# Attention and a rational MoE layer on one core: one store per bank at the end, low weight parts made in place, another order of banks at the start

## The chip, the cores and the metric

The kernel runs on one core of a Trainium2 chip. The metric is the device time of one execution in microseconds. PE is the matrix engine (TensorE), DVE the vector engine (VectorE), ACT the scalar engine (ScalarE), POOL is GpSimd and SP the sync engine, which only issues transfers. PSUM, where matmuls write, has eight banks of 512 fp32 columns by 128 partitions.

## What is computed

Attention over 8 batches, 8 heads, 576 tokens and a head size of 64, in two forms that are added, and then a layer with a rational activation over the 4608 tokens:

```python
def _attn_ref(q, k, v):              # (8, 8, 576, 64)
    q_d, k_d, v_d = (mean over groups of 4 tokens)
    out_up = np.repeat(softmax(q_d @ k_d.T / 8) @ v_d, 4, axis=2)
    mask = np.abs(pos[:, None] - pos[None, :]) < 4
    out_local = softmax(where(mask, q @ k.T / 8, -1e9)) @ v
    return out_up + out_local

def _moe_ref(x, w_in, w_out, a, b):  # (4608, 512), (512, 2048), (2048, 512)
    h = x @ w_in
    P = a[0] + a[1] * h + a[2] * h**2 + a[3] * h**3
    Q = 1.0 + abs(b[0]) * abs(h) + abs(b[1]) * h**2
    return (P / (Q + 1e-06)) @ w_out
```

## The kernel before

The tokens form nine blocks of 512: the first 512 tokens of each batch, and one block of the 64 remaining tokens of all eight batches. A block is worked off in 16 steps, one per 128 columns of `w_in` (an "fc"). Step n has three parts: `h_part` writes h(n) into one PSUM bank (PE), `middle` makes the activation from it (four ACT operations that read the bank, two more, and seven DVE operations), which leaves a high part `gh` and a low part `gl` (tiles g0 to g3), and `o_part`, called o(n), multiplies them by the matching 128 rows of `w_out` and adds into four banks, `ob` (banks 4 to 7), over the 16 steps. o(n) stands two steps behind h(n). At the end of a block `store` copies the four banks to SBUF and issues their stores.

Products run as three passes of a rounded format (fp32r): high times high, low times high, high times low. So every weight pair of two fc (128 x 1024 elements) exists as a high part `wh` and a low part `wl`; `weights` makes them from 64-bit words that SP loads (tiles sx, sl): ACT scales a word (line 367), DVE puts the two halves together (370, 373), ACT casts the high part (403) and DVE subtracts to get the low part (406). `w_out` takes this way. `w_in` does not at once: in block 0 (`NAT` = 16 steps) h is one pass of plain fp32 from the exact weights `wb`, with x in fp32 (line 911), four matmuls of 512 columns. After every second step `parts` turns the exact pair that block 0 no longer needs into `wh` and `wl` for the later blocks: before, `wb` lies in the place of `wh`, ACT writes the negated rounded value to `wl` (428), a transfer issued by POOL adds `wb` to it (415), and ACT rounds `wb` in place (430).

The attention of a batch goes by pairs of heads: local scores, a maximum, exponentials (tile el), the same for the pooled form (tiles pq, epc), a division, transposes on PE and copies by ACT back to SBUF (et, eptc), products with v and, by `put_x`, the sum of both forms into x (tile xf). Two pairs make a `Half`; `turn` is the transposes, `weight` the products with v (part_b, part_a). Batch 0 has nothing to overlap with and runs first, its halves over four pairs of banks `bp[0]` to `bp[3]`; batch 1 runs beside block 0, batch 2 beside block 1, and so on.

The order of instructions on every engine is fixed beforehand: each piece of work is handed to a planner (`Plan`) with an assumed duration, its readers and writers, and a due time, and the planner lists the pieces engine by engine. Due times come from constants at the end of the file (`H0`, `H_FIRST`, `H_STEP`, `QUAD_GAP`). While PE would wait in batch 0 the planner's caller adds `warm` matmuls (line 1128) that write an idle bank and are not used.

Of the kernel before, what the change touches and what calls it, by code (L numbers as in the profile page):

```python
# [9 lines left out]
F32 = mybir.dt.float32  # L10
# [9 lines left out]
DM, DF = 512, 2048  # L20
# [167 lines left out]
def attention_moe(  # L188
# [49 lines left out]
    for name, parts in (("wl", low2), ("wh", high2)):  # L238
        for w in range(2):
            for f in range(0, NFC, 2):  # L240
                t = put(f"{name}{w}_{f}", [P, 2, NCC, P], F32R)
                parts[w].append(t)
                if (parts is high2) == (f < (0 if w else NAT)):
                    bits2[w][f // 2] = put(f"wb{w}_{f}", [P, 2, NCC, P], I32, t.at)
    high, low = (
        [[part(x[w][f // 2], x[w][f // 2].ap[:, f % 2], f % 2 * 4 * DM, 4 * DM) for f in range(NFC)] for w in range(2)]
# [104 lines left out]
    def weights(w, f, spot, due=None):  # L351
        st = spot.ap.rearrange("p n (c f two) -> p n c f two", two=2, c=NCC)
        whole = f < (0 if w else NAT)
        added = not whole and ADDED[w] <= f < NFC - 2
        room = low2[w][f // 2 + 1] if added else (high2 if whole else low2)[w][f // 2]
        word = aside[w][f // 2 + 1] if added else bits2[w][f // 2]

        def load():
            src = w_in[f : f + 2] if w == 0 else w_out[f * P : (f + 2) * P, :].rearrange("(n p) x -> n p x", p=P)
            nc.sync.dma_start(out=spot.ap, in_=src.rearrange("n p x -> p n x"))  # L360

        word1, word0 = st[:, :, :, :, 1], st[:, :, :, :, 0]
# [14 lines left out]

        add("SP", 3.3, load, (), (spot,), due=due)
        add("ACT", 0.94, scaled, (spot,), (spot,))
        add("DVE", 0.6, upper, (spot,), (room,))  # L380
        add("DVE", 1.13, lower, (spot, room), (room,))
        if added:
            hi, lo = high2[w][f // 2], low2[w][f // 2]
            if f >= CAST:
                add(
                    "POOL", 1.0, lambda: nc.gpsimd.dma_start(out=flat2(hi), in_=flat2(word).bitcast(F32)),
                    (room,), (hi,), lag=CLAG, load=3.0,
                )
            else:
                add("ACT", 0.88, lambda: nc.scalar.copy(out=hi.ap, in_=word.ap.bitcast(F32)), (room,), (hi,))  # L390
            if NEG:
                add(
                    "DVE", 0.6,
                    lambda: nc.vector.tensor_single_scalar(
                        out=lo.ap, in_=hi.ap.bitcast(F32), scalar=-1.0, op=ALU.mult
                    ), (hi,), (lo,),
                )
            else:
                add("ACT", 0.88, lambda: nc.scalar.mul(out=lo.ap, in_=hi.ap.bitcast(F32), mul=-1.0), (hi,), (lo,))
            accumulate(lo, word, room)  # L400
        elif not whole:
            hi, lo = high2[w][f // 2], low2[w][f // 2]
            add("ACT", 0.88, lambda: nc.scalar.copy(out=hi.ap, in_=word.ap.bitcast(F32)), (lo,), (hi,))
            add(
                "DVE", 1.13,
                lambda: nc.vector.tensor_tensor(
                    out=lo.ap, in0=word.ap.bitcast(F32), in1=hi.ap.bitcast(F32), op=ALU.subtract
                ),
                (lo, hi), (lo,),
            )  # L410
# [8 lines left out]
    def parts(w, f, due=None):  # L419

        hi, lo, word = high2[w][f // 2], low2[w][f // 2], bits2[w][f // 2]
        exact = word.ap.bitcast(F32)
        if DEFER == 2:
            add("ACT", 0.88, lambda: nc.scalar.mul(out=lo.ap, in_=exact, mul=-1.0), (hi,), (lo,), due=due)
            accumulate(lo, word, hi, due)
            add("DVE", 0.6, lambda: nc.vector.tensor_copy(out=hi.ap, in_=exact), (hi,), (hi,), due=due)
        elif DEFER == 1:
            add("ACT", 0.88, lambda: nc.scalar.mul(out=lo.ap, in_=exact, mul=-1.0), (hi,), (lo,), due=due)
            accumulate(lo, word, hi, due)
            add("ACT", 0.88, lambda: nc.scalar.copy(out=hi.ap, in_=exact), (hi,), (hi,), due=due)  # L430
        else:
            add("ACT", 0.88, lambda: nc.scalar.mul(out=lo.ap, in_=exact, mul=-1.0), (hi,), (lo,), due=due)
            add(
                "DVE", 1.13, lambda: nc.vector.tensor_tensor(
                    out=lo.ap, in0=exact, in1=lo.ap.bitcast(F32), op=ALU.add
                ), (hi, lo), (lo,), due=due,
            )
            add("DVE", 0.6, lambda: nc.vector.tensor_copy(out=hi.ap, in_=exact), (hi,), (hi,), due=due)
# [172 lines left out]
    def normalize(c):  # L611
# [10 lines left out]
                    scale=sm[:, NW + i : NW + i + 1],  # L622
                )

        if c.b in EP_DVE:
            add(
                "DVE", 0.6,
                lambda: nc.vector.tensor_tensor(
                    out=c.pool.e.ap[:, :, :, c.odd, :QC], in0=c.pool.e.ap[:, :, :, c.odd, :QC],
                    in1=sm[:, NW:].unsqueeze(2).unsqueeze(3).broadcast_to([P, NQ, NK, QC]), op=ALU.mult,  # L630
                ),
                (*c.eproom, s.sm), c.eproom,
            )
        else:
            add("ACT", 0.92, pooled, (*c.eproom, s.sm), c.eproom, lag=LATE)
# [263 lines left out]
    def h_part(n, f):  # L899
# [5 lines left out]
        if n < NAT:  # L905

            x = xsf[blk.slot][1]
            for c in range(NCC):

                def issue(c=c):  # L910
                    nc.tensor.matmul(  # L911
                        ph.ap, lhsT=bits2[0][fc // 2].ap[:, fc % 2, c, :].bitcast(F32), rhs=x.ap[:, c, :],
                        start=(c == 0), stop=(c == NCC - 1),
                    )

                add("PE", 0.858, issue, (high[0][fc], part(x, None, 4 * c * t, 4 * t)), (ph,), due=due_h(n) + 0.05 * c)
            return
        for part_ in range(3):
            i, j = PROD[part_]
# [81 lines left out]
    def store(k):  # L1001
        blk = blocks[k]
        due = due_h(blk.first + blk.nstep + 2)
        for sub in range(blk.nsub):
            po = ob[sub]
            hi, osb = blk.x[0], xsf[blk.slot][0]
            room = part(hi, None, 4 * sub * DM, 4 * DM)
            osb = flat(osb.ap)[:, sub * DM : (sub + 1) * DM]
            if k == len(blocks) - 1 and sub % 2:
                add("DVE", 0.6, lambda osb=osb, po=po: nc.vector.tensor_copy(out=osb, in_=po.ap), (po,), (room,), due=due)  # L1010
            else:
                add("ACT", 0.49, lambda osb=osb, po=po: nc.scalar.copy(out=osb, in_=po.ap), (po,), (room,), due=due)
            if blk.b is not None:
                rows = [(blk.b, sub * P, P)]
            else:
                rows = blk.rows[2 * sub : 2 * sub + 2]
            for i, (b, t, n) in enumerate(rows):
                add(
                    "SP", 0.7,
                    lambda osb=osb, b=b, t=t, n=n, i=i: nc.sync.dma_start(  # L1020
                        out=out[b * S + t : b * S + t + n, :], in_=osb[i * n : (i + 1) * n, :]
                    ),
                    (room,), (), due=due + 2,
                )
# [9 lines left out]


    due0 = due_h(0) - 4.0
    firsts = [Half(0, q, due0 - 10.0 * (1 - q)) for q in range(2)]
    c0 = [c for x in firsts for c in x.cs]
    for c, due in zip(c0, LOADS[0]):
        load_qk(c, due)  # L1040
# [20 lines left out]
        half_.turn(bp[a], bp[b], bp[a])  # L1061
        half_.weight(bp[b], bp[a])

    begin(c0[0], 0)
    begin(c0[1], 1)
    begin(c0[2], 3)
    for c in c0[:2]:
        pool_qk(c)
    firsts[0].pooled(bp[2])
    begin(c0[3], 0)  # L1070
    for c in c0[2:]:
        pool_qk(c)
    firsts[1].pooled(bp[1])
    finish(firsts[0], 2, 3)
    finish(firsts[1], 0, 1)
    for w, f, spot in chunks[len(early) :]:
        weights(w, f, spot)

# [105 lines left out]
ADDED = (99, 99)
# [67 lines left out]
```

## Time and profile before

| | |
|---|---|
| time, three runs | 961.51, 961.99, 962.8 us; median 961.99 |
| the profiled execution | 961.83 us, span 960.0 us |
| granted clock of PE | 0.996 in the mean |
| busy | PE 939.1, weight load 738.1, DVE 843.4, ACT 812.4, POOL 121.1 us |
| instructions | 19318 |
| moved | read 74.37 MB, written 9.44 MB |

The span goes from the first to the last instruction; the execution's own time is 1.8 us longer. In a row of the profile stand the line, the engine, the operation, what it writes and reads (tile names, without numbers), the shape, the count, and behind the bar busy time, mean of one, and the idle time before it with what ended it. PEld is the loading of weights into PE, which runs beside the matmuls. A busy PE includes pipelining, so its busy time is not its work. An fp32 matmul (line 911) shows as two records.

### The profile page before, as it was taken

To read this page: it belongs to the slowest core of one execution; us is meant where nothing else is said; L and a number is where in the kernel's file an instruction comes from. 1 tells how busy PE (TensorE), PEld (TensorE's weight loads), DVE (VectorE), ACT (ScalarE), POOL (GpSimd) and SP (SyncE) were. 2 spreads that over 40 slices of the span, in tenths; PEclk is the share of its full clock that TensorE was granted. 3 is DMA by queue.
4 is the path that set the end of the run, shared out by engine and by line. 5 is a ranking of instruction groups with operands and counts; after the bars stand their busy time and mean duration, and the time that the engine had idled before them with its cause. 6 is when DMAs were issued, how large, how long until landed. Compare 5 with 4: busy or idle time off the path is not lost.

```text
span 960.0 us, 19318 instructions
## 1 busy us (share of the span) xinstructions
PE 939.1 (98%) x7184; PEld 738.1 (77%) x7184; DVE 843.4 (88%) x1430; ACT 812.4 (85%) x1992; POOL 121.1 (13%) x144
## 2 busy tenths in 40 slices
PE   7899999999999999999999999999999999999996
PEld 5565667878878788888878887878878888888885
DVE  7799999898889889798988898898979899988885
ACT  4799999999798888979797979888897977778674
POOL 1212022121102020212121210212021000000000
PEclk9999999999999999999999999999999999999999
DMA  9997477363333444343343423434332010001001
GB/s 298 279 326 194 105 191 175 84 123 84 72 99 62 108 69 110 63 107 58 94 93 76 89 58 110 74 93 77 102 57 51 1 45 1 1 1 45 1 0 45
DMA packets 44318, 89.26 MB, mean 93 GB/s; under 512 B 4992, under 2 KB 25856, under 8 KB 44224
## 3 DMA queue, kind: packets, MB, share of 16 engines
q1 hardware_dynamic: 25344, 63.52, 20.1%
q0 software_dynamic: 18880, 24.50, 17.7%
q8 instruction: 57, 0.93, 0.4%
q14 instruction: 37, 0.30, 0.1%
HBM read 74.37 MB, written 9.44 MB: 87 GB/s over the span
## 4 chain that ended last, share of the span: by engine, by line
PE 58%; ACT 20%; DVE 17%; issue 4%; DVEq 0%; POOL 0%; ACTq 0%; POOLq 0%
PE psum L989 26%; PE psum L923 25%; ACT m L936 6%; ACT el L739 4%; ACT epc L603 2%; DVE g L963 2%; DVE m L966 2%; DVE m L971 2%; ACT gb L936 2%; DVE g L972 2%; PE psum L911 2%; DVE m L951 1%; ACT epc L620 1%; DVE m L956 1%; DVE m L960 1%
## 5 line engine op out<-in xcount | busy, mean ns | idle before, releaser
L989 PE MATMUL psum<-wh,g 128*128 128x512 f32 x1152 | 392.2, 402 | 3.2 <-DVE g L972 1.4
L936 ACT ACTIVATE m<-psum,cf 128x512 f32<-128x512 f32 x288 | 216.0, 754 | 62.6 <-PE psum L923 54.8
L923 PE MATMUL psum<-xs,wh 128*128 128x512 f32 x1024 | 260.6, 394 | 0.0
L989 PEld LDWEIGHTS psum<-wh,g 128*128 128x128 f32 x1152 | 213.6, 188 | 55.7 <-DVE g L972 5.0
L989 PE MATMUL psum<-wl,g 128*128 128x512 f32 x576 | 224.3, 390 | 0.0
L923 PEld LDWEIGHTS psum<-xs,wh 128*128 128x128 f32 x1024 | 189.5, 188 | 42.2 <-issue 1.8
L963 DVE TENSOR_TENSOR g<-m,m 128x512 fp32r<-128x512 f32 x144 | 99.3, 690 | 65.7 <-ACT m L936 60.3
L923 PE MATMUL psum<-xs,wl 128*128 128x512 f32 x512 | 138.3, 392 | 0.0
L989 PEld LDWEIGHTS psum<-wl,g 128*128 128x128 f32 x576 | 108.2, 188 | 24.7 <-issue 2.2
L936 ACT ACTIVATE gb<-psum,cf 128x512 f32<-128x512 f32 x144 | 116.8, 811 | 10.4 <-PE psum L989 10.3
L936 ACT ACTIVATE gb<-m,cf 128x512 f32<-128x512 f32 x144 | 108.5, 754 | 19.6 <-DVE m L951 12.8
L474 POOL DMA_DIRECT2D pq<-in_qkp_dram x84 | 74.4, 929 | 383.5 <-DMA pq<-in_qkp_dram 305.0
L951 DVE SCALAR_TENSOR_TENSOR m<-m,cf,m 128x512 f32<-128x512 f32 x144 | 107.3, 745 | 6.9 <-ACT m L936 6.9
L923 PEld LDWEIGHTS psum<-xs,wl 128*128 128x128 f32 x512 | 95.4, 188 | 20.4 <-issue 0.6
L936 ACT ACTIVATE m<-gb 128x512 f32<-128x512 f32 x144 | 93.8, 651 | 19.4 <-DVE m L956 17.7
L960 DVE TENSOR_TENSOR m<-m,gb 128x512 f32<-128x512 f32 x144 | 99.0, 688 | 7.4
L966 DVE SCALAR_TENSOR_TENSOR m<-m,g 128x512 f32<-128x512 f32 x144 | 99.3, 690 | 3.4
L972 DVE TENSOR_TENSOR g<-m,m 128x512 fp32r<-128x512 f32 x144 | 98.7, 685 | 4.0
L971 DVE TENSOR_TENSOR m<-m,m 128x512 f32<-128x512 f32 x144 | 99.1, 688 | 2.6
L956 DVE TENSOR_TENSOR m<-m,m 128x512 f32<-128x512 f32 x144 | 98.5, 684 | 2.8 <-ACT m L936 2.8
L936 ACT ACTIVATE m<-psum 128x512 f32<-128x512 f32 x144 | 88.8, 617 | 0.0
L474 POOL DMA_DIRECT2D vpc<-in_vp_dram x42 | 34.9, 830 | 216.3 <-DMA vpc<-in_vp_dram 201.8
(78 smaller groups left out, 950.2 us busy)
## 6 DMA issues: line engine op xcount, KB each, us to landing
qk<-in_qk_dram SPq DMA_DIRECT2D x32, 590.0 KB, 3.9
pq<-in_qkp_dram POOLq DMA_DIRECT2D x84, 144.0 KB, 3.4
vw<-in_vw_dram SPq DMA_DIRECT2D x32, 320.0 KB, 4.0
out_dram<-xf SPq DMA_DIRECT2D x32, 256.0 KB, 2.4
vpc<-in_vp_dram POOLq DMA_DIRECT2D x42, 168.0 KB, 3.7
sx<-in_w_in_dram SPq DMA_DIRECT2D x5, 1024.0 KB, 12.2
sl<-in_w_out_dram SPq DMA_DIRECT2D x4, 1024.0 KB, 12.5
sx<-in_w_out_dram SPq DMA_DIRECT2D x4, 1024.0 KB, 6.5
```

Of the source, the lines that this page charges most:

```text
L474: lambda d=dst, x=x: nc.gpsimd.dma_start(out=d.ap, in_=x, accum_op=ALU.add),
L739: nc.scalar.activation(out=e[:, n], in_=e[:, n], func=AF.Exp, bias=nm[:, n : n + 1], scale=scale, accum_out=sm[:, n : n + 1],)
L923: nc.tensor.matmul(ph.ap[:, f * t : (f + 1) * t], lhsT=(high, low)[j][0][fc].ap[:, c, :], rhs=blk.x[i].ap[:, c, :] if blk.b is not None el ...
L936: add("ACT", cost, lambda: nc.scalar.activation(out=out_.ap, in_=in_, func=func, **kw), (room_in, cf, *more), (out_,))
L951: lambda: v.scalar_tensor_tensor(out=tb.ap, in0=tq.ap, scalar=b1, in1=tb.ap, op0=ALU.mult, op1=ALU.add),
L956: add("DVE", 0.61, lambda: v.tensor_tensor(out=ta.ap, in0=ta.ap, in1=tq.ap, op=ALU.mult), (ta, tq), (ta,))
L960: add("DVE", 0.61, lambda: v.tensor_tensor(out=ta.ap, in0=ta.ap, in1=u.ap, op=ALU.add), (ta, u), (ta,))
L963: add("DVE", 0.61, lambda: v.tensor_tensor(out=gh.ap, in0=ta.ap, in1=tq.ap, op=ALU.mult), (ta, tq), (gh,))
L966: lambda: v.scalar_tensor_tensor(out=tb.ap, in0=tb.ap, scalar=CONE, in1=gh.ap.bitcast(F32), op0=ALU.add, op1=ALU.mult),
L971: add("DVE", 0.61, lambda: v.tensor_tensor(out=tb.ap, in0=ta.ap, in1=tb.ap, op=ALU.subtract), (ta, tb), (tb,))
L972: add("DVE", 0.61, lambda: v.tensor_tensor(out=gl.ap, in0=tb.ap, in1=tq.ap, op=ALU.mult), (tb, tq), (gl,))
L989: nc.tensor.matmul(ob[sub].ap, lhsT=g[i].ap[:, f0 : f0 + P], rhs=flat((high, low)[j][1][fc].ap), start=(fc == 0 and m == 0), stop=(fc == N ...
```

## The change

Four things change.

1. `store` for the last block: ACT copies the left half of each output bank and DVE the right half, and each bank's 128 rows, which belong to two batches, go out in one transfer instead of two, on the queues of SP and ACT in turn (sub 0 and 2, sub 1 and 3).
2. `DEFER` goes from 1 to 4: the exact pair lies in the place of `wl`, ACT casts it to `wh` (now line 424), and DVE subtracts in place (line 426). There is no transfer.
3. Batch 0's pairs use other banks (`BANKS`), h(0) and h(1) stand in banks 2 and 3 instead of 7 and 5 (`HFIRST`), where h(2) and h(3) follow, and due times differ.
4. `EP_DVE` is asked by pair instead of by batch, with the four pairs of batch 0 in it.

```diff
@@ parts
+        if DEFER == 4:
+            add("ACT", 0.88, lambda: nc.scalar.copy(out=hi.ap, in_=exact), (lo,), (hi,), due=due)
+            add(
+                "DVE", 1.13, lambda: nc.vector.tensor_tensor(
+                    out=lo.ap, in0=exact, in1=hi.ap.bitcast(F32), op=ALU.subtract
+                ), (lo, hi), (lo,), due=due,
+            )
@@ store
-            if k == len(blocks) - 1 and sub % 2:
-                add("DVE", 0.6, lambda osb=osb, po=po: nc.vector.tensor_copy(out=osb, in_=po.ap), (po,), (room,), due=due)
...
+            if blk.b is None:
+                lo, hi = (osb[:, i * DM // 2 : (i + 1) * DM // 2] for i in range(2))
+                plo, phi = (po.ap[:, i * DM // 2 : (i + 1) * DM // 2] for i in range(2))
+                rooms = [part(room, None, i * 2 * DM, 2 * DM) for i in range(2)]
+                add("ACT", 0.3, lambda o=lo, p=plo: nc.scalar.copy(out=o, in_=p), (po,), (rooms[0],), due=due)
+                add("DVE", 0.34, lambda o=hi, p=phi: nc.vector.tensor_copy(out=o, in_=p), (po,), (rooms[1],), due=due)
+                dst = out.rearrange("(b s) d -> b s d", s=S)[2 * sub : 2 * sub + 2, FULL:, :]
+                queue, engine = ("SP", nc.sync) if sub % 2 == 0 else ("ACT", nc.scalar)
                 add(
-                    "SP", 0.7,
...
+                    queue, 0.7, lambda e=engine, d=dst, o=osb: e.dma_start(out=d, in_=o), (room,), (),
+                    due=due + 2 + sub,
                 )
@@ batch 0
-    begin(c0[0], 0)
-    begin(c0[1], 1)
-    begin(c0[2], 3)
...
-    firsts[0].pooled(bp[2])
-    begin(c0[3], 0)
...
-    firsts[1].pooled(bp[1])
-    finish(firsts[0], 2, 3)
-    finish(firsts[1], 0, 1)
+    begin(c0[0], turns[0])
+    begin(c0[1], turns[1])
...
+    firsts[0].pooled(bp[pooled[0]])
...
+    begin(c0[3], turns[3])
...
+    firsts[1].pooled(bp[pooled[1]])
+    finish(firsts[0], *ends[0])
+    finish(firsts[1], *ends[1])
@@ constants
-HFIRST = (7, 5)
+HFIRST = (2, 3)
-H0 = 14.21
+H0 = 20.18
...
+BANKS = ((0, 1, 3, 2), (2, 3), ((0, 1), (2, 3)))
...
-DEFER = 1
+DEFER = 4
```

What the constants do to the order shows in the lists of the engines. ACT in batch 0, before, from the pooled exponentials of half 0 (epc0) on; el2 and el3 are the local exponentials of pairs 2 and 3, epc1 the pooled ones of half 1, et and eptc the copies of transposes of half 0:

```order
L603 ACTIVATE epc0_162,sm1_157<-psum,nm1_153 128x3x48 x3
L553 ACTIVATE el2_178<-psum 128x5x64
L553 ACTIVATE el3_183<-psum 128x5x64
L553 ACTIVATE el2_178<-psum 128x5x64
L553 ACTIVATE el3_183<-psum 128x5x64
L367 ACTIVATE sx0_189<-sx0_189 128x1024
L796 COPY eptc0_163<-psum 112x384
L796 COPY et0_168<-psum 128x512
L796 COPY et1_173<-psum 128x512
L796 COPY eptc0_163<-psum 112x384
L603 ACTIVATE epc1_185,sm2_158<-psum,nm2_154 128x3x48 x3
L603 ACTIVATE epc1_185,sm3_159<-psum,nm3_155 128x3x48 x3
```

ACT at the same place now, from the first copy on:

```order
L803 COPY eptc0_163<-psum 112x384
L803 COPY et0_168<-psum 128x512
L803 COPY et1_173<-psum 128x512
L803 COPY eptc0_163<-psum 112x384
L560 ACTIVATE el3_183<-psum 128x5x64
L610 ACTIVATE epc1_185,sm2_158<-psum,nm2_154 128x3x48 x3
L803 COPY et0_168<-psum 128x128
L803 COPY et1_173<-psum 128x128
L803 COPY eptc0_163<-psum 112x96
L560 ACTIVATE el3_183<-psum 128x5x64
L367 ACTIVATE sx1_190<-sx1_190 128x1024
L610 ACTIVATE epc1_185,sm3_159<-psum,nm3_155 128x3x48 x3
```

Pair 3 (el3, sm3) has moved behind the copies of half 0, and the pooled exponentials of half 1 are no longer made in one piece ahead of the last three copies.

DVE at the start of block 1, before; m, g and gb are tiles of the activation:

```order
L963 TENSOR_TENSOR g0_138<-m0_132,m4_136 128x512
L406 TENSOR_TENSOR wl1_14_78<-wb1_14_79,wh1_14_103 128x1024
L966 SCALAR_TENSOR_TENSOR m2_134<-m2_134,g0_138 128x512
L956 TENSOR_TENSOR m1_133<-m1_133,m5_137 128x512
L971 TENSOR_TENSOR m2_134<-m0_132,m2_134 128x512
L960 TENSOR_TENSOR m1_133<-m1_133,gb1_143 128x512
L972 TENSOR_TENSOR g2_140<-m2_134,m4_136 128x512
L963 TENSOR_TENSOR g1_139<-m1_133,m5_137 128x512
```

DVE at the same place now:

```order
L978 TENSOR_TENSOR m2_134<-m0_132,m2_134 128x512
L963 TENSOR_TENSOR m1_133<-m1_133,m5_137 128x512
L979 TENSOR_TENSOR g2_140<-m2_134,m4_136 128x512
L967 TENSOR_TENSOR m1_133<-m1_133,gb1_143 128x512
L426 TENSOR_TENSOR wl0_2_58<-wb0_2_59,wh0_2_89 128x1024
L970 TENSOR_TENSOR g1_139<-m1_133,m5_137 128x512
```

A subtraction for `w_in` (line 426) stands between two operations of a step, directly ahead of a g; six more follow in the next twelve steps, most at the same place.

PE ahead of the first o (the rows with g0), before; wb0_0 holds fc 0 and 1, wb0_2 fc 2 and 3, and qk0 is a pair of batch 1:

```order
L911 MATMUL psum<-xf0_1_123,wb0_2_83 128x512
L911 MATMUL psum<-xf0_1_123,wb0_0_81 128x512 x4
L911 MATMUL psum<-xf0_1_123,wb0_2_83 128x512 x3
L495 LDWEIGHTS identb_147
...
L505 MATMUL psum<-qk0_164 64x64 x20
L911 MATMUL psum<-xf0_1_123,wb0_2_83 128x512
L989 MATMUL psum<-wh1_0_96,g0_138 128x512
```

PE at the same place now:

```order
L502 LDWEIGHTS identb_147
...
L512 MATMUL psum<-qk0_164 64x64 x20
L918 MATMUL psum<-xf0_1_123,wb0_0_57 128x512 x4
L918 MATMUL psum<-xf0_1_123,wb0_2_59 128x512 x4
L996 MATMUL psum<-wh1_0_96,g0_138 128x512
```

Batch 1's first scores have moved ahead of the second half of h(0) and h(1), and of fc 2 and 3 four matmuls stand ahead of the first o instead of five.

More of the change, by code (lines that the diff above doesn't have):

```diff
@@ L242, in attention_moe @@
                 parts[w].append(t)
-                if (parts is high2) == (f < (0 if w else NAT)):
+                if (parts is high2) == (f < (0 if w else NAT) and DEFER != 4):
                     bits2[w][f // 2] = put(f"wb{w}_{f}", [P, 2, NCC, P], I32, t.at)
@@ L354, in weights @@
         added = not whole and ADDED[w] <= f < NFC - 2
-        room = low2[w][f // 2 + 1] if added else (high2 if whole else low2)[w][f // 2]
+        room = low2[w][f // 2 + 1] if added else (high2 if whole and DEFER != 4 else low2)[w][f // 2]
         word = aside[w][f // 2 + 1] if added else bits2[w][f // 2]
@@ L422, in parts @@
         exact = word.ap.bitcast(F32)
-        if DEFER == 2:
+        if DEFER == 4:
[5 more added lines that the diff above has]
+            )
+        elif DEFER == 2:
             add("ACT", 0.88, lambda: nc.scalar.mul(out=lo.ap, in_=exact, mul=-1.0), (hi,), (lo,), due=due)
@@ L623, in pooled @@
                 )
-        if c.b in EP_DVE:
+        if c.p in EP_DVE:
             add(
@@ L914, in issue @@
                     )
-                add("PE", 0.858, issue, (high[0][fc], part(x, None, 4 * c * t, 4 * t)), (ph,), due=due_h(n) + 0.05 * c)
+                add("PE", 0.858, issue, ((low if DEFER == 4 else high)[0][fc], part(x, None, 4 * c * t, 4 * t)), (ph,), due=due_h(n) + 0.05 * c)
             return
@@ L1005, in store @@
             po = ob[sub]
-            hi, osb = blk.x[0], xsf[blk.slot][0]
-            room = part(hi, None, 4 * sub * DM, 4 * DM)
+            xhi, osb = blk.x[0], xsf[blk.slot][0]
+            room = part(xhi, None, 4 * sub * DM, 4 * DM)
             osb = flat(osb.ap)[:, sub * DM : (sub + 1) * DM]
-            if k == len(blocks) - 1 and sub % 2:
-                add("DVE", 0.6, lambda osb=osb, po=po: nc.vector.tensor_copy(out=osb, in_=po.ap), (po,), (room,), due=due)
-            else:
-                add("ACT", 0.49, lambda osb=osb, po=po: nc.scalar.copy(out=osb, in_=po.ap), (po,), (room,), due=due)
@@ L1013, in store @@
[L1013 to L1017, printed above, removed]
-                add(
-                    "SP", 0.7,
[L1020 to L1023, printed above, removed]
-                )
+            if blk.b is None:
[6 more added lines that the diff above has]
+                queue, engine = ("SP", nc.sync) if sub % 2 == 0 else ("ACT", nc.scalar)
+                add(
+                    queue, 0.7, lambda e=engine, d=dst, o=osb: e.dma_start(out=d, in_=o), (room,), (),
+                    due=due + 2 + sub,
+                )
+                continue
@@ L1027, in attention_moe @@
+            add("ACT", 0.49, lambda osb=osb, po=po: nc.scalar.copy(out=osb, in_=po.ap), (po,), (room,), due=due)
+            add(
+                "SP", 0.7,
+                lambda osb=osb, b=blk.b, t=sub * P: nc.sync.dma_start(out=out[b * S + t : b * S + t + P, :], in_=osb),
+                (room,), (), due=due + 2,
+            )
     order = sorted(((w, f) for w in range(2) for f in range(0, NFC, 2)), key=lambda c: c[1] / 2 + 1.5 * c[0])
@@ L1036, in attention_moe @@
     due0 = due_h(0) - 4.0
-    firsts = [Half(0, q, due0 - 10.0 * (1 - q)) for q in range(2)]
+    firsts = [Half(0, q, due0 - LEAD * (1 - q)) for q in range(2)]
     c0 = [c for x in firsts for c in x.cs]
@@ L1062, in finish @@
         half_.weight(bp[b], bp[a])
-    begin(c0[0], 0)
-    begin(c0[1], 1)
-    begin(c0[2], 3)
+    turns, pooled, ends = BANKS
+    begin(c0[0], turns[0])
+    begin(c0[1], turns[1])
+    if FOURTH == 0:
+        begin(c0[2], turns[2])
     for c in c0[:2]:
         pool_qk(c)
-    firsts[0].pooled(bp[2])
-    begin(c0[3], 0)
+    firsts[0].pooled(bp[pooled[0]])
+    if FOURTH == 1:
+        begin(c0[2], turns[2])
+    begin(c0[3], turns[3])
     for c in c0[2:]:
         pool_qk(c)
-    firsts[1].pooled(bp[1])
-    finish(firsts[0], 2, 3)
-    finish(firsts[1], 0, 1)
+    firsts[1].pooled(bp[pooled[1]])
+    finish(firsts[0], *ends[0])
+    finish(firsts[1], *ends[1])
     for w, f, spot in chunks[len(early) :]:
@@ L1162 @@
 NAT = 16
-HFIRST = (7, 5)
+HFIRST = (2, 3)
 LAG = 2
 O_LAG = 2.09
-H0 = 14.21
-H_FIRST = 6.11
-H_STEP = 6.25
+H0 = 20.18
+H_FIRST = 5.88
+H_STEP = 6.23
 SPLIT_EARLY = 9.53
-QUAD_GAP = 43.57
+QUAD_GAP = 36.94
 WARM = 0.6
-EP_DVE = (0,)
+EP_DVE = (0, 1, 2, 3)
+LEAD = 14.49
+FOURTH = 0
+BANKS = ((0, 1, 3, 2), (2, 3), ((0, 1), (2, 3)))
 SPOTS = (0, 1, 2, 3, 4, 5)
@@ L1177 @@
 ALAG = 6.5
-DEFER = 1
+DEFER = 4
 CAST = 99
 CLAG = 6.0
-DEFERRED = -12.08
+DEFERRED = -27.61
 NEG = 1
```

## The prediction

> **What bounds the kernel now.** I read the table by stage first, then the head and the tail in order of time, then the groups of the operations that the change touches.
>
> Busy time by stage (columns: stage, length, then busy us and instruction count of PE, PEld, DVE, ACT, POOL; granted clock, DMA share, GB/s):
>
> ```profile
> 0.00:40.00 40.00, 31.62 (x574) 23.54 (x574) 31.40 (x58) 22.79 (x63) 8.04 (x14) 0.96 0.91 289
> 40.00:160.00 120.00, 116.78 (x838) 72.90 (x839) 115.12 (x190) 114.48 (x269) 25.10 (x28) 1.00 0.76 205
> 160.00:260.00 100.00, 99.86 (x800) 80.74 (x799) 89.02 (x158) 92.17 (x246) 17.41 (x20) 1.00 0.46 100
> 260.00:760.00 500.00, 498.69 (x4036) 402.68 (x4035) 436.28 (x767) 438.98 (x1186) 70.57 (x82) 1.00 0.37 80
> 760.00:951.00 191.00, 191.00 (x937) 157.58 (x935) 170.34 (x260) 142.92 (x229) 0.00 (x0) 1.00 0.03 12
> 951.00:960.00 9.00, 1.20 (x5) 0.67 (x4) 1.29 (x2) 1.07 (x2) 0.00 (x0) 0.80 0.51 117
> ```
>
> From 40 to 951 PE is busy for 906.3 of 911 us: matmuls set the time, and the change leaves the useful ones as they are. In 40 to 160 DVE and ACT are at 96 and 95%, so there three engines are about equally tight; from 160 on DVE has 11% free. Room outside PE's own work is in the first 40 us, where PE waits for batch 0, and in the 9 us behind the last matmul.
>
> **The tail.** Last matmuls, the copies of the four output banks, their stores, and, for comparison, the four stores of an ordinary block:
>
> ```profile
> 951.04 1.17 PE L989 MATMUL psum<-wh,g 128*128 128x512 f32 x4
> 951.54 1.07 ACT L1012 COPY xf<-psum 128x512 f32<-128x512 f32 x2 [3.62 <-PE psum L989]
> 951.78 1.29 DVE L1010 COPY xf<-psum 128x512 f32<-128x512 f32 x2 [0.89 <-PE psum L989]
> 952.16 5.18 SPq L1020 DMA_DIRECT2D out_dram<-xf  x8
> ...
> 870.75 1.81 SPq L1020 DMA_DIRECT2D out_dram<-xf  x4
> ```
>
> DMA share in 40 slices, of 870 to 875 us (slices of 0.125 us), then of 951 to 960 us (0.225 us):
>
> ```profile
> DMA  0000000000003899989999999999999999500000
> ```
>
> ```profile
> DMA  0000000000597997987299599697897977000000
> ```
>
> Both stores move 1.05 MB. The ordinary four need 870.75 to 874.38, 3.63 us from the first issue to the last byte, with the engines full. The eight of the last block need 952.16 to 958.65, 6.49 us, with gaps: eight issues in a row take SP 5.18 us, 0.65 each, and they set the pace. So with half as many issues the transfer itself becomes the limit and the last byte comes 3.63 us after the first issue.
>
> That first issue comes later. A bank is now copied in two halves, by ACT and then by DVE (the DVE half waits for ACT's). Prices of 256 columns lie between these rows:
>
> ```profile
> L796 ACT COPY et<-psum 128x512 f32<-128x512 f32 x32 | 18.0, 647 | 0.0
> L796 ACT COPY et<-psum 128x128 f32<-128x128 f32 x32 | 7.4, 306 | 0.0
> L670 DVE TENSOR_TENSOR xf<-psum,up 128x464 f32<-128x464 f32 x32 | 18.9, 631 | 0.2
> L670 DVE TENSOR_TENSOR xf<-psum,up 128x64 f32<-128x64 f32 x32 | 6.0, 215 | 0.0
> ```
>
> Interpolated: 0.42 us on either engine (ends: 0.31 to 0.65). The first bank is whole at 951.54 + 0.42 + 0.06 + 0.42 = 952.44, 0.3 us after before's first issue. Later banks follow each 0.35 us or so, faster than the 0.69 us that a store's bytes take, so neither queue starves. Last byte: 952.45 + 3.63 = 956.1 against 958.65, a gain of 2.5 us; what follows (the landing and the closing barrier, 960.0 - 958.65) stays. Bounds: 3.2 us if nothing but the 5.18 us of issuing counted and it fell to two issues per queue with the 2.3 us of landing that both rows of stores show; 1.6 us if the first store from ACT's queue, of which the trace has none, starts one slow issue (0.65) and one copy (0.3) later. I take 2.5.
>
> The Trainium skill speaks against part of this. "DMA: Bandwidth & Descriptors", Issuing engines are not separate DMA queues, says that queues share the sixteen engines and a second one only saves issue time: by it the four stores from SP alone would do the same. The row at 870.75 agrees: one queue fills the engines. And "PSUM — Partial Sum Buffer", PSUM bank collisions raise a hardware error, says that two engines must not read one bank at once, so that halving a bank between ACT and DVE buys no parallel copy; were they parallel, the tail would gain 2.9.
>
> **The head.** Half 0 is pairs 0 and 1 of batch 0, half 1 pairs 2 and 3. ACT, then PE, DVE and ACT in order of time, and PE's granted clock:
>
> ```profile
> 24.26 0.38 ACT L603 ACTIVATE epc<-psum,nm 128x144 f32<-128x144 f32 x1 [0.36 <-DVE nm L597]
> ...
> 26.05 0.40 ACT L603 ACTIVATE epc<-psum,nm 128x144 f32<-128x144 f32 x1
> 26.71 0.29 ACT L796 COPY eptc<-psum 112x96 f32<-112x96 f32 x1
> ```
>
> ```profile
> 21.53 1.54 DVE L561 TENSOR_REDUCE sm<-el 128x10 f32<-128x640 f32 x2
> ```
>
> ```profile
> 27.06 1.39 PE L819 MATMUL psum<-eptc,vf 48*64 48x144 f32 x32 [2.15 <-ACT eptc L796]
> 28.21 2.37 PE L649 MATMUL psum<-et,vw 64*64 64x58 f32 x80
> ...
> 38.08 1.34 PE L649 MATMUL psum<-et,vw 64*64 64x58 f32 x80
> ```
>
> ```profile
> 28.00:31.40 3.40, 3.40 (x97) 3.29 (x87) 3.33 (x7) 3.00 (x7) 1.17 (x2) 0.50 0.92 300
> ```
>
> ```profile
> 39.56 1.68 DVE L670 TENSOR_TENSOR xf<-psum,up 128x48 f32<-128x48 f32 x6 [0.37 <-ACT up L843]
> 40.04 3.67 PE L911 MATMUL psum<-xf,wb 128*128 128x512 f32 x8 [0.62 <-DVE xf L670]
> 42.95 0.69 ACT L936 ACTIVATE m<-psum,cf 128x512 f32<-128x512 f32 x1 [3.43 <-PE psum L911]
> ```
>
> Before, ACT makes six pooled exponentials of half 1 (0.36 apart, 24.26 to 26.41) and only then the last copies of half 0, for which PE waits 2.15 us; behind this wait PE runs at half clock for 3.4 us, and the same 80 matmuls take 2.37 instead of 1.34 us. After, three of the six stand ahead of those copies (-1.07), and one of the two sums (1.54 for two) has left DVE's way to them (-0.7), while one local exponential came in ahead (+0.4) and hides in ACT's wait: PE starts 24.26 - 0.6 + 1.07 + 0.6 = 25.4 instead of 27.06. Sixteen added warm matmuls fill its waits, so I count no dip of the clock: 1.0 us on those 80, and part_a of half 0 ends near 28.3 instead of 30.6. Pair 3, which now comes last, holds this back a little: its three exponentials stand behind one weight scaling (1.04) on ACT. Followed through ACT's and DVE's rows by the same durations, half 1's last x comes at 37.4 to 39.05 instead of 39.56 to 41.24: 2.0 us. So ACT's first operation of step 0 moves from 42.95 to about 40.95.
>
> Against this, h(0) to h(3) now share two banks instead of four. h(2) waits until ACT has read h(0), four operations, 2.4 us from 42.95 to the row at 45.34:
>
> ```profile
> 43.54 0.59 ACT L936 ACTIVATE m<-psum 128x512 f32<-128x512 f32 x1
> 44.02 0.78 ACT L936 ACTIVATE m<-psum,cf 128x512 f32<-128x512 f32 x1
> 44.68 0.79 ACT L936 ACTIVATE gb<-psum,cf 128x512 f32<-128x512 f32 x1
> 45.34 0.73 ACT L936 ACTIVATE gb<-m,cf 128x512 f32<-128x512 f32 x1
> ...
> 48.48 0.80 PE L989 MATMUL psum<-wh,g 128*128 128x512 f32 x1
> ```
>
> PE has done h(0) and h(1) by 42.4 and idles to 40.95 + 2.4 = 43.4; h(2) ends and o(0) starts near 46.9 instead of 48.48, with one fp32 product (0.86; eight passes take 3.67 at 40.04) less behind it. PE's own lead is 0.8 us, that of ACT and DVE 2.0. Since all three are tight up to 160, I take the middle, 1.3 (ends 0 and 2.5).
>
> **The low parts.** For eight pairs of fc blocks a negation and a cast on ACT and an accumulating DMA become a cast on ACT and a subtraction on DVE:
>
> ```profile
> L428 ACT ACTIVATE wl<-wb 128x1024 fp32r<-128x1024 f32 x8 | 8.4, 1077 | 0.0
> L415 POOL DMA_DIRECT2D wl<-wb x8 | 9.2, 1227 | 0.0
> L406 DVE TENSOR_TENSOR wl<-wb,wh 128x1024 fp32r<-128x1024 f32 x8 | 9.8, 1220 | 1.5 <-ACT wh L403 1.4
> L963 DVE TENSOR_TENSOR g<-m,m 128x512 fp32r<-128x512 f32 x144 | 99.3, 690 | 65.7 <-ACT m L936 60.3
> ```
>
> ACT loses 8 x 1.08 = 8.6 us, POOL and the DMA engines 8 transfers of 0.5 MB (off the path: no compute engine waits for them), DVE gains 8 x 1.22 = 9.8. By place: one subtraction falls in step 0, one in step 15, six in steps 16 to 26. Counted in DVE's list from step 0's first operation to step 16's, two subtractions (2.4 us) come in, two score reductions (one now ahead of step 0, one behind step 16) and one operation of a step go out (0.8 each by the busy time of such rows): nothing on balance; ACT's list loses six negations and gains three casts, 3 us less. No cost there. From 160 to 260 DVE goes from 89 to about 96 of 100 us, and ACT from 92 to 85. At 96% in 40 to 160 PE lost 3.2 us in 120; here it loses 0.1 in 100. So the cost lies between 0 and 2.6 us. What speaks for the low end is L963: before each g DVE idles 0.46 us (65.7 / 144) for ACT, and the subtractions stand just there, with an ACT that has less to do. I take 0.8. `EP_DVE` selects the same four pairs as before: nothing.
>
> **The sum.** -2.5 - 1.3 + 0.8 = -3.0 us against the profiled 961.83 (span 960.0, 1.8 around it); the median of the runs is 961.99, 0.16 more. Prediction 958.9, span near 957.
>
> **Rivals.** (a) Slower: each subtraction in steps 16 to 26 stands in front of g, so that it pushes g by 1.22 - 0.46 = 0.8 us and PE, whose lead over DVE is two steps, runs dry. All of it exposed: 8 x 1.22 = 9.8, 962 - 3.8 + 9.8 = 968. It decides from 3.8 us on, four tenths of the work. Against it: PE kept 99.9% there with DVE at 89%, and ACT is relieved. With the result slower than before: 0.08. (b) The head gives nothing: two banks take back what half 1 wins, or PE's instruction stream stalls elsewhere; with the cost of the low parts between 0.8 and 1.5 that gives 962 - 2.5 + 0.8 to 1.5 = 960.3 to 961: 0.22. (c) The head's 2.0 us carry through and the subtractions fill idle DVE: 962 - 2.5 - 2.0 = 957.5, with a tail at its best 956.8: 0.25. (d) The change does not do what it says in the tail: the store from ACT's queue starts late, gain 1.6 instead of 2.5: 959.8, inside my forecast's spread. My forecast, with (d): 0.45, 958 to 960.
>
> 0.2% is 1.9 us, about what this kernel's measurement can tell from no change: faster means below 960.1. Mine and (c) lie there, 0.70; most of (b) is the same, 0.22; slower 0.08. The range 956.4 to 961.3 takes in (c) and (b) and leaves out (a).
>
> **What would show it.** Right: four stores, the last byte about 3.6 us after the first issue; ACT's first step operation near 41 us; a clock of 1.00 in 28 to 31.4; PE's busy share in 160 to 260 still above 98.5%; eight L426 rows of 1.22 us. Wrong: waits of PE for g of DVE in steps 16 to 30 that sum to over 2 us, a first step operation at 42.5 or later, or a gap in the DMA share of the last stores.

## The result: slower by 1.5%

| | before | after |
|---|---|---|
| median of five runs | 961.99 us (960.38 to 965.11) | 977.22 us (976.59 to 977.71) |
| profiled execution | 961.83 us, span 960.0 | 977.49 us, span 975.5 |

The ratio is 1.0154 (95% interval 1.0134 to 1.0174). Forecast were 958.9 us, 956.4 to 961.3. The loss of 15.2 us lies wholly behind the last matmuls, which come earlier than before.

### The profile page after: what moved, and what is told of

Its sections match the earlier page's. It is cut to its first block, busy times and chain, and to the rows that moved or that the text cites. A ratio compares the mean times of both kernels' runs of the same rounds, so it can differ in the third digit from the quotient of the medians.

```text
span 975.5 us, 19334 instructions
## 1 busy us (share of the span) xinstructions
PE 938.5 (96%) x7200; PEld 738.4 (76%) x7200; DVE 848.4 (87%) x1440; ACT 804.4 (82%) x1986; POOL 113.9 (12%) x136
## 4 chain that ended last, share of the span: by engine, by line
PE 69%; ACT 14%; DVE 9%; issue 3%; DMA 2%; DVEq 0%; SPq 0%; ACTq 0%
PE psum L996 31%; PE psum L930 29%; ACT m L943 4%; ACT gb L943 2%; ACT el L746 2%; DMA sx<-in_w_in_dram 2%; PE psum L656 2%; PE psum L826 1%; DVE m L973 1%; DVE g L970 1%; PE psum L766 1%; ACT epc L610 1%; DVE m L978 1%; PE psum L772 1%; DVE m L963 1%
## 5 line engine op out<-in xcount | busy, mean ns | idle before, releaser
L943 ACT ACTIVATE m<-gb 128x512 f32<-128x512 f32 x144 | 94.0, 653 | 18.7 <-DVE m L963 17.1
L918 PE MATMUL psum<-xf,wb 128*128 128x512 f32 x128 | 59.7, 599 | 0.9 <-ACT gb L943 0.9
```

Of the source, the lines that this page charges most:

```text
L918: nc.tensor.matmul(ph.ap, lhsT=bits2[0][fc // 2].ap[:, fc % 2, c, :].bitcast(F32), rhs=x.ap[:, c, :], start=(c == 0), stop=(c == NCC - 1),)
L943: add("ACT", cost, lambda: nc.scalar.activation(out=out_.ap, in_=in_, func=func, **kw), (room_in, cf, *more), (out_,))
```

## The profile after

Busy time by stage of the changed kernel (stage, length, then busy us and count of PE, PEld, DVE, ACT, POOL; granted clock, DMA share, GB/s); the first row is the stretch in which PE ran at half clock before:

```profile
28.00:31.40 3.40, 2.15 (x26) 1.90 (x18) 3.33 (x11) 3.07 (x10) 0.00 (x0) 1.00 0.66 187
...
0.00:40.00 40.00, 32.45 (x635) 24.29 (x636) 32.20 (x60) 22.81 (x63) 6.65 (x13) 1.00 0.92 288
40.00:160.00 120.00, 116.41 (x761) 73.60 (x762) 118.53 (x193) 113.72 (x269) 22.08 (x25) 1.00 0.64 183
160.00:260.00 100.00, 100.00 (x841) 80.98 (x840) 92.90 (x162) 85.74 (x238) 14.74 (x18) 1.00 0.39 85
260.00:760.00 500.00, 499.06 (x4038) 402.62 (x4037) 434.63 (x768) 439.42 (x1188) 70.42 (x82) 1.00 0.36 79
```

The clock is 1.00 in every row, also where it was 0.50 before, and PE is full from 160 us on, a little more than before. Now the tail in order of time (start, duration, engine; stores are the rows with DMA_DIRECT2D):

```profile
949.41 1.15 PE L996 MATMUL psum<-wh,g 128*128 128x512 f32 x4
949.92 1.20 ACT L1020 COPY xf<-psum 128x256 f32<-128x256 f32 x4 [3.63 <-PE psum L996]
950.33 1.42 DVE L1021 COPY xf<-psum 128x256 f32<-128x256 f32 x4 [1.06 <-ACT xf L1020]
950.78 1.29 SPq L1025 DMA_DIRECT2D out_dram<-xf  x2
951.11 1.71 ACTq L1025 DMA_DIRECT2D out_dram<-xf  x2
```

PE reaches its last four matmuls at 949.41, 1.63 us earlier than before (951.04). This is one profile of each: in those of the five runs below that share the order ahead of the tail they come between 947.60 and 949.58, in the two that share the order before at 950.64 and 951.11. The copies and the first issue follow as forecast. But the span ends at 975.5: from those matmuls to the end it takes 26.1 us instead of 8.96. So 960.0 - 1.63 + 17.1 = 975.5. The transfers of 949 to 975.5 us (40 slices of 0.66 us; the third row counts packets by size) show why:

```profile
DMA  0000011111111111111111111111111111111000
GB/s 0 0 0 0 12 12 37 25 43 49 49 56 49 49 56 49 49 49 56 49 49 49 56 49 49 53 53 49 49 56 49 49 49 56 49 49 53 34 0 0
DMA packets 521, 1.06 MB, mean 40 GB/s; under 512 B 8, under 2 KB 8, under 8 KB 520
```

The same bytes as before trickle out at 49 GB/s, with a tenth of the DMA engines' time busy. The small packets (under 512 B) count the engines at work, as the runs below bear out: 8 for four stores, two each. Before, the same row of the tail is:

```profile
DMA packets 641, 1.06 MB, mean 96 GB/s; under 512 B 128, under 2 KB 128, under 8 KB 640
```

128 for eight stores, sixteen each. The share of the sixteen engines says the same when it is read in the middle of the transfer: 0.13 x 16 = 2.

```profile
956.00:970.00 14.00, 0.00 (x0) 0.00 (x0) 0.00 (x0) 0.00 (x0) 0.00 (x0) 0.50 0.13 51
```

What is special in the changed store is the shape on its DRAM side, 2 x 64 x 512: two batches, 64 rows, 512 columns. Before, it was 64 x 512. That the outermost size, 2, sets the number of engines is theory A below; its rivals are ACT's queue (B) and the number of dimensions (C).

## The experiments

**All four stores on SP.** `queue, engine = "SP", nc.sync` for every bank.

> The changed kernel with all four stores of the last block issued by SP; nothing else differs. Theory A (two engines): each store's address pattern on the DRAM side is 2 x 64 x 512, and a transfer is spread over as many DMA engines as its outermost dimension allows, here 2 of 16; the queue that issues it does not matter. Then the data still move at the 49 GB/s of the changed kernel, 1.05 MB take 21 us, and the time stays at 977 us (976 to 979). Theory B (the scalar engine's queue): the stores issued by ACT are what is slow. Then it falls to the time first forecast, 958 to 960 us. Theory C (three dimensions): any pattern of three dimensions on the DRAM side is slow, whatever its sizes; here as A.

Measured: 977.27 us, ratio 1.0151 (1.0130 to 1.0171). Theory B is out: without ACT's queue nothing changes.

**One store per batch, on the two queues.**

```diff
-                dst = out.rearrange("(b s) d -> b s d", s=S)[2 * sub : 2 * sub + 2, FULL:, :]
+                for i, (b, t, n) in enumerate(blk.rows[2 * sub : 2 * sub + 2]):
+                    queue, engine = (("SP", nc.sync), ("ACT", nc.scalar))[i]
...
+                            out=out[b * S + t : b * S + t + n, :], in_=o[i * n : (i + 1) * n, :]
```

> The changed kernel with each bank's store split into one store per batch (64 rows of 512, eight stores, the first of a bank on SP and the second on ACT, four for each queue). Theory A: the outermost dimension is 64, all 16 engines take part, the 1.05 MB pass in about 3 us, and with four issues of 0.65 us on each queue the last byte comes 3.6 to 4.4 us after the first issue at 950.8; span about 956, time 957.7 to 958.7 us. Theory B: half the bytes still go through ACT's queue, so most of the loss stays: over 970 us. Theory C: two dimensions, as A.

Measured: 959.10 us, ratio 0.9962 (0.9950 to 0.9975). With an outermost size of 64 the loss is gone, with half of the bytes still on ACT's queue. A and C both say so. (The median is 0.4 over the expected band; the profiled execution took 957.36.)

**62 and 51 rows.** The same kernel, but each store leaves out the last rows of its 64, so that the pattern keeps two dimensions:

```diff
-  out=out[b * S + t : b * S + t + n, :], in_=o[i * n : (i + 1) * n, :]
+  out=out[b * S + t : b * S + t + 62, :], in_=o[i * n : i * n + 62, :]
```

> As the run with one store per batch on two queues, but each store moves 62 of the 64 rows (the last two rows of each batch's 64 are left out). The pattern has two dimensions, 62 x 512. Theory A: the largest number up to 16 that divides 62 is 2, so two engines again: 1.02 MB at 49 GB/s are 20.7 us, time about 976 to 978 us, though it moves fewer bytes than the run with 64 rows. Theory C, and any theory in which the count of rows does not matter: as with 64 rows, 957.5 to 959 us.

> As the run with 62 rows for each store, with 51 rows (thirteen rows of each batch's 64 are left out). Theory A in its form with divisors: the largest number up to 16 that divides 51 is 3, so three engines at the 24.5 GB/s that each of two showed, 73 GB/s: 0.836 MB take 11.4 us, tail from the first store to the end about 14.5 us, time 964 to 967. If any count of rows that is not a multiple of 16 fell back to two engines: 17 us, time 970 to 973. If only very small counts were spread badly: 957 to 959.

Measured, one run each: 975.87 us with 62 rows and 967.97 with 51. Packets of the tail with 62 rows, eight stores:

```profile
DMA packets 514, 1.03 MB, mean 39 GB/s; under 512 B 16, under 2 KB 16, under 8 KB 512
```

and with 51 rows; below it the middle of that transfer (DMA share and GB/s are the last two columns):

```profile
DMA packets 435, 0.86 MB, mean 39 GB/s; under 512 B 24, under 2 KB 24, under 8 KB 432
...
956.00:962.00 6.00, 0.00 (x0) 0.00 (x0) 0.00 (x0) 0.00 (x0) 0.00 (x0) 0.50 0.20 77
```

16 / 8 = 2 engines for 62 rows, 24 / 8 = 3 for 51, and 0.20 x 16 = 3.2. Taking two rows in 64 away costs 17 us (975.87 against 959.10). Theory C cannot explain it: these patterns have two dimensions. The time with 51 rows is 1 us over the band of A: from the first store to the end of the span it takes 15.1 us instead of some 14.5, since the first 3 us of the transfer run below the 73 GB/s that were counted on.

**One store per bank, with all engines.** The tokens of a bank's two batches alternate, so that the rows come outermost:

```diff
-  rhs=blk.x[i].ap[:, c, :] if blk.b is not None else tails(blk.x[i], c).ap,
+  rhs=blk.x[i].ap[:, c, :] if blk.b is not None
+      else tails(blk.x[i], c).ap.rearrange("p (q b) t -> p q t b", b=2),
...
-  dst = out.rearrange("(b s) d -> b s d", s=S)[2 * sub : 2 * sub + 2, FULL:, :]
+  dst = out.rearrange("(b s) d -> b s d", s=S)[2 * sub : 2 * sub + 2, FULL:, :].rearrange("b t d -> t b d")
```

> The changed kernel with one store per bank still, but the tokens of the last block in another order: the moving operand of h reads the two batches of a bank alternately, so row p of a bank is token p/2 of batch p%2, and the store's DRAM pattern is 64 x 2 x 512 instead of 2 x 64 x 512. Same four stores, same bytes, same 2048-byte rows, same three dimensions. Theory A (engines by the outermost dimension): 64 allows all 16, so the tail is the one that was forecast: last byte 3.6 us after the first issue, time 957 to 958.5 us, about 19 us faster than the changed kernel. Theory C (any pattern of three dimensions is slow): still about 977. A cost of its own would be matmuls of the last block whose moving operand is read with a stride; then the stages before 947 grow.

Measured: 957.63 us, ratio 0.9949 (0.9935 to 0.9963). Its tail (transfers of 947 to 955.7 us in slices of 0.2175 us, then a stretch in the middle):

```profile
947.98 1.17 PE L997 MATMUL psum<-wh,g 128*128 128x512 f32 x4
...
949.34 1.33 SPq L1026 DMA_DIRECT2D out_dram<-xf  x2
949.67 1.29 ACTq L1026 DMA_DIRECT2D out_dram<-xf  x2
```

```profile
DMA  0000000000000000199999999999960000000000
GB/s 0 0 0 0 0 0 0 0 0 0 0 0 0 0 0 0 66 386 367 386 358 414 358 396 358 433 330 395 339 217 28 19 9 0 0 0 0 0 0 0
DMA packets 577, 1.06 MB, mean 121 GB/s; under 512 B 64, under 2 KB 64, under 8 KB 576
...
950.50:953.40 2.90, 0.00 (x0) 0.00 (x0) 0.00 (x0) 0.00 (x0) 0.00 (x0) 0.74 0.96 356
```

Three dimensions again, so C is out; four stores, 2048-byte rows: 64 / 4 = 16 engines, a share of 0.96 and 356 GB/s instead of 51. The run is 20 us faster than the changed kernel: 18.4 of it is the tail (7.7 us from the last four matmuls to the end instead of 26.1), and the rest comes ahead of it, with the order in which the tokens are read (below). Per engine the rates are alike: 356 / 15.4, 77 / 3.2 and 51 / 2.1 GB/s are 23 to 24.

That is theory A, and the Trainium skill states it, in "DMA: Bandwidth & Descriptors", Why a DMA increments its semaphore by 16 and not by 1: the number of engines of a transfer is the largest number up to 16 that divides the outermost dimension over 1 of the address patterns on both sides. The runs here agree for 2, 62, 51 and 64, with 2, 2, 3 and 16 engines.

**The same with SP alone.**

> The run with paired tokens in the last block, with all four stores issued by SP. Forecast's step (the transfer is the limit, sixteen engines full, whichever queue): same as with two queues, 957.6 us (957 to 958.3). Rival: the second queue hides issue time: 0.6 to 1.3 us more, 958.2 to 959.

Measured: 957.55 us, ratio 0.9948 (0.9931 to 0.9965), the same as with two queues. The second queue is worth nothing here.

**The parts of the change alone.** First the changed kernel with the old store, then the changed store on the kernel before:

> The changed kernel with the store of the kernel before (whole bank copies, eight stores of 64 rows on SP); the new order of banks and the in-place low parts stay. Every theory of the tail: the last output step starts 1.6 us earlier than in the kernel before (947.4 against 949.05) and the tail is the old 10.95 us, so the time is 962.0 - 1.65 = 960.3 us (959.9 to 960.8). If the new head and low parts cost something that the profile of the changed kernel hides, it is 961.5 or more.

> The kernel before with the changed store alone (halves of each bank copied by ACT and DVE, one store of 2 x 64 x 512 per bank on SP and ACT). Theory A: the tail from the last output step's start takes 28.1 us as in the changed kernel instead of 10.95, so 962.2 + 17.1 = 979.3 us (978.5 to 980). If head or low parts had a share in the loss it would be nearer to 962.

Measured: 960.22 us, ratio 0.9975 (0.9963 to 0.9987), and 980.05 us, 1.0185 (1.0169 to 1.0202). The two parts add up: the old store keeps what head and low parts bring, the new store costs its 17 us on either kernel. Then the repaired tail alone (one store per batch on two queues, on the kernel before):

> The kernel before with only its last store changed, in a form in which all sixteen engines take part (halves of a bank copied by ACT and DVE; one store per batch of 64 rows, four on SP and four on ACT). The forecast's step for the tail: 2.5 us less, 959.6 us. What the traces of the repaired tails read (from the last four matmuls to the end of the span 7.6 to 7.8 us, against 8.96 before): 1.2 us less, 960.9 us (960.4 to 961.4).

Measured: 961.03 us, ratio 0.9991 (0.9981 to 1.0001), 1.15 less by the medians, with an interval that just reaches zero (-1.8 to +0.1): the 2.5 of the forecast lies outside it. Then the in-place low parts alone (the DEFER lines of the diff on the kernel before), and the new order of batch 0 alone (the changed kernel with the old store and `DEFER = 1`):

> The kernel before with the low parts alone made in place (a cast on ACT and a subtraction on DVE, eight times, with the changed due time), old head, old store. The forecast's step: +0.8 us, so 963.0 (962 to 964.6). Rival: ACT's relief counts and the subtractions lie in DVE's idle time: -0.2 to -1 us, 961.2 to 962.

> The changed kernel with the old store and the old way of making low parts (negation, accumulating transfer, cast): only the new order of banks and the due times of batch 0 and after stay. The forecast's step: -1.3 us, 960.9 (959.7 to 962.2). The trace of the changed kernel shows the first output step 0.9 us earlier and the last 1.65 us earlier: if the whole of that comes from the order, 960.5; if the later 0.75 comes from the low parts, 961.3.

Measured: low parts 964.54 us, ratio 1.0017 (1.0006 to 1.0027), so +1.6; head 960.27 us, ratio 0.9979 (0.9970 to 0.9989), so -2.0. For the head, the reading that all of the 1.65 us comes from the order (960.5) is the nearer. For the low parts the rival's gain did not come: alone they cost twice what was forecast (the interval, +0.6 to +2.6, takes in the 0.8 too), and with the new head (960.22 against 960.27) nothing that shows. The profiles say the same from the first o to the last four matmuls: 902.56 us before, 904.17 with the low parts alone, 902.00 with the head alone, 901.64 with both. The stage in which most of the low parts fall, in the low parts alone:

```profile
160.00:260.00 100.00, 99.04 (x792) 79.93 (x793) 93.77 (x164) 87.11 (x239) 14.63 (x17) 1.00 0.35 77
```

DVE is as busy as in the changed kernel (93.8 against 92.9), but PE is idle for 0.96 us, 0.8 more than before (99.86 of 100). Both of PE's waits in this stage, and between them a place where two of the subtractions stand back to back on DVE (in the changed kernel with the old store there is a step between any two):

```profile
160.67 1.19 PE L930 MATMUL psum<-xs,wh 128*128 128x512 f32 x4 [0.74 <-ACT gb L943]
...
169.87 2.36 DVE L426 TENSOR_TENSOR wl<-wb,wh 128x1024 fp32r<-128x1024 f32 x2
...
172.88 0.50 PE L996 MATMUL psum<-wh,g 128*128 128x512 f32 x1 [0.21 <-DVE g L970]
```

The pair is not the main cost: behind it PE waits 0.21 us, but 0.74 us come nine microseconds ahead of it, where h waits for ACT's last read of its bank. No run moved either, so what costs the +1.6 stays open.

**A reading order that is faster.** The paired run was 1.6 us better before its tail: the last four matmuls come at 947.98 instead of 949.41, though step 128, the first of the last block, starts 0.16 us later. From the first h of this step to the last four matmuls it takes 91.75 us in all eleven profiles in which the last block is read in order, and 90.15 in the four in which h alone is read as in the paired run. Matmuls of the last block in 872 to 946 us, of the changed kernel and of the paired one (busy, mean ns of one):

```profile
L930 PE MATMUL psum<-xs,wh 128*128 128x512 f32 x104 | 25.7, 389 | 0.0
```

```profile
L930 PE MATMUL psum<-xs,wh 128*128 128x512 f32 x104 | 24.6, 379 | 0.0
```

The mean includes the pipeline; the starts are 226.7 ns apart with the moving operand read in order, and 215.8 ns with it read alternately from two places 1 KB apart (192 matmuls, 43.52 and 41.44 us). So the order was taken to all h products, and then to o as well:

```diff
-  rhs=x.ap[:, c, :],
+  rhs=x.ap[:, c, :].rearrange("p (a t) -> p t a", a=2),
...
-  rhs=flat((high, low)[j][1][fc].ap),
+  rhs=flat((high, low)[j][1][fc].ap).rearrange("p (a d) -> p d a", a=2),
```

> The run with paired tokens, with the same reading order in all blocks: the moving operand of every h matmul takes its 512 columns alternately from two runs 1 KB apart (token t, then token t + 256), and the stores of all blocks put the rows back (pattern 64 x 2 x 512). In the run with paired tokens the 192 matmuls of the last block so read started 215.8 ns apart instead of 226.7 (41.44 us instead of 43.52). Theory E (the order of reading sets the interval): 7 x 192 more matmuls save 10.9 ns each, 14.6 us, less some 0.5 us a block by which the matmuls of o beside them grew, so 957.6 - 11 = 946.5 us (943 to 949); block 0's plain fp32 matmuls may add up to 2.6. Theory F (something of the last block alone, such as its runs of 64 tokens): no change, 957 to 958.5. If ACT and DVE (88% busy) become the limit, in between.

> As the run before, and the moving operand of o (rows of w_out, 512 columns) is read in the same alternating order too; the copies out of PSUM put the columns back, with a stride of 8 bytes. Theory E: 1728 matmuls of o save 10.9 ns each, 18.8 us, so 946.5 - 18.8 = 928 us at best; up to 940 if ACT and DVE, which then need 5.5 of 5.95 us a step, become the limit or the copies with a stride cost more. Theory F: no change against the run before.

Measured: 960.78 us, ratio 0.9982 (0.9970 to 0.9994), and 968.29 us, 1.0060 (1.0040 to 1.0080). Both missed theory E's numbers, though the interval of 216 ns is there in the h products of blocks 1 to 8 and, in the second run, in those of o. Groups of the whole execution, block 0's plain fp32 matmuls before and with pairs everywhere:

```profile
L911 PE MATMUL psum<-xf,wb 128*128 128x512 f32 x128 | 60.0, 597 | 2.0 <-DVE wb L373 0.7 <-ACT gb L936 0.7 <-DVE xf L670 0.6
```

```profile
L918 PE MATMUL psum<-xf,wb 128*128 128x512 f32 x128 | 73.8, 709 | 1.1 <-DVE xf L677 0.6 <-ACT gb L944 0.5
```

Plain fp32 gets slower by the order that makes the rounded format faster: 540 ns from record to record instead of 429. Block 0 lost 9 us by it. With o, the copies that put the columns back take nearly twice as long. They write alternately to two places 1 KB apart; the "stride of 8 bytes" of the expectation is wrong (all blocks' copies of a bank, in the paired run and with pairs in o too):

```profile
L1030 ACT COPY xf<-psum 128x512 f32<-128x512 f32 x32 | 16.5, 619 | 0.1
```

```profile
L1030 ACT COPY xf<-psum 128x512 f32<-128x512 f32 x32 | 30.9, 1143 | 0.0
```

That is 14 us more on ACT, and PE's idle time ahead of o grows from 5.6 to 20.9 us, most of it waits for g and for these copies (pairs everywhere, then pairs in o too):

```profile
L997 PE MATMUL psum<-wh,g 128*128 128x512 f32 x1152 | 395.2, 404 | 5.6 <-DVE g L971 3.0 <-DVE g L980 2.5
```

```profile
L997 PE MATMUL psum<-wh,g 128*128 128x512 f32 x1152 | 383.7, 394 | 20.9 <-DVE g L980 5.8 <-DVE g L971 5.7 <-ACT xf L1030 4.7
```

That the copies alone cost the gain was not tried.

So the last run keeps the order for h of blocks 1 to 8 alone:

> The run with paired tokens everywhere, but block 0, whose h products are plain fp32, reads its tokens in order again; blocks 1 to 8 keep the alternating order. In the run with pairs everywhere the fp32 records of block 0 came 540 ns apart instead of 429, and its block 0 lost 9 us, while from step 32 to step 128 it was 4.6 us faster. If block 0 was the loss and the reading order holds: 957.6 - 4.6 = 953.0 us (952 to 954.5). If the gain of the rounded blocks is taken back by waits for DVE and ACT: 955 to 957.6.

Measured: 951.85 us, ratio 0.9894 (0.9878 to 0.9909): 10 us faster than the kernel before and 25 faster than the changed one, 0.15 under the expected band. In blocks 1 to 7 the order saves 5.8 us by the medians (4.7 by the spans) out of the 14.6 that its matmuls could save. One part of the rest is that o now waits for g, 4.5 us more in the stretch shown; another that o's own matmuls start 230 ns apart in the median instead of 227, for which no run gives the reason. Group of o in 260 to 760 us, paired last block alone and blocks 1 to 8 (behind the second bar the idle time):

```profile
L997 PE MATMUL psum<-wh,g 128*128 128x512 f32 x616 | 208.9, 399 | 0.9 <-DVE g L980 0.9
```

```profile
L997 PE MATMUL psum<-wh,g 128*128 128x512 f32 x619 | 210.9, 400 | 5.4 <-DVE g L971 2.8 <-DVE g L980 2.5
```

## Why the prediction was wrong

**The tail: the step that failed.** "So with half as many issues the transfer itself becomes the limit and the last byte comes 3.63 us after the first issue." The first half is true, and more than was meant. The 3.63 us came from an ordinary block's four stores, whose DRAM side is 128 x 512, and were given to stores of 2 x 64 x 512 because the bytes, the count and the rows of 2048 bytes agree. That all sixteen engines work on either was assumed, not read; on two of them the 1.05 MB took about 22 us, and the time from the last four matmuls to the end, 6.4 us by the forecast, was 26.1. The prediction named "a gap in the DMA share of the last stores" as what would prove it wrong; the share is what does, though it is no gap. The rival (d), a late store on ACT's queue, had the wrong mechanism: SP's stores were as slow. What it took from the Trainium skill ("DMA: Bandwidth & Descriptors", Issuing engines are not separate DMA queues) held: with all engines at work SP alone does the same (957.55 against 957.63). The chance of 0.08 for a slower kernel was given to the subtractions of (a), which are not what made it slower.

**The size behind that.** With all engines the tail brings 1.2, not 2.5: from the last four matmuls to the end it takes 7.7 us in the paired run (955.7 - 947.98), 7.6 with SP alone and 7.8 with one store per batch, against 8.96. The copies are right (first issue 1.36 us after the last matmuls' start, forecast 1.41). But full engines end only 4.1 us after the first issue, thin traffic runs to 4.8, and the end of the span comes 1.5 us behind that. The forecast's 3.63 + 1.35 is 1.4 short.

**The head: right in direction, sizes mixed.** PE's 48 products start at 25.26 (forecast 25.4, though its sum gives 25.3), the dip of the clock is gone. PE's row, ACT's first step operation, PE's wait for the two banks and the first o of the changed kernel:

```profile
25.26 1.70 PE L826 MATMUL psum<-eptc,vf 48*64 48x144 f32 x48
...
41.91 0.69 ACT L943 ACTIVATE m<-psum,cf 128x512 f32<-128x512 f32 x1 [2.71 <-PE psum L918]
...
44.47 3.70 PE L918 MATMUL psum<-xf,wb 128*128 128x512 f32 x8 [0.94 <-ACT gb L943]
...
47.60 0.79 PE L996 MATMUL psum<-wh,g 128*128 128x512 f32 x1
```

The wait for the two banks is as forecast (0.94 us against 1.0). 41.91 against the forecast 40.95 and 47.60 against 46.9 are half of the gain of x and half of that of o in this profile, but one profile cannot tell: in the nine others with this head and block 0 read in order the first o comes between 45.98 and 48.12, and in the four with the old head between 48.23 and 48.74. The forecast's 46.9 lies inside. The head alone gives -2.0 (interval -2.9 to -1.1, which takes in the -1.3), inside the ends 0 and -2.5. In its profile the first o comes 1.2 us earlier than before (47.31 against 48.48) and the last four matmuls 1.7 (949.31 against 951.04): about half a microsecond is won after step 0, which the working by step 0 alone could not see.

**The low parts: duration right, cover not.** Eight rows of 1.22 us as forecast (9.8 us, mean 1223). The +0.8 is nothing that shows with the new head and +1.6 with the old; the rival of +9.8 did not come. In sum, head and low parts with the old store are 960.2 measured against 961.5 by the forecast's terms (961.99 - 1.3 + 0.8).

## What to carry to other kernels

Before you merge transfers, look at the outermost size of both address patterns: bytes, row length and count of stores say nothing of how many engines work, and a permutation of two dimensions took 18 us off the tail here. Read it off the profile: small packets per store, or the DMA share in the middle of the transfer times sixteen. A duration may be taken from another row only if the shape that sets the parallelism is the same.

## What the runs showed of the hardware that was not expected

- 51 rows are stored faster than 62, and 64 faster than both; the count's divisors decide, not the bytes.
- Two queues did not add engines: with stores of two engines each on SP and ACT, and with all of them on SP, the share in the middle of the transfer is 0.13 and the rate 51 GB/s.
- A rounded (fp32r) matmul of 512 columns takes 215.8 ns from start to start when its moving operand alternates between two places 1 KB apart, and 226.7 ns when it is read in order; plain fp32 goes the other way, 540 against 429 ns a record. Why was not tried. The Trainium skill, "TensorE: Matmul & The Clock Gate", Back-to-back issue gap, gives 518 cycles for 512 columns as the gap of isolated matmuls; at its 2.4 GHz that is an estimate of 215.8 ns. The alternate reading reached it, in streams of matmuls, and reading in order did not in any run here.
- A copy by ACT out of PSUM that writes alternately to two places 1 KB apart (columns put back) took 1143 ns instead of 619.
